# A transformer block with linear attention and a gated MLP: x^T of half the tiles by VectorE transposes of 4-byte elements and transfers inside SBUF

## The chip, the cores and the metric

The kernel runs on one core of a Trainium2 chip. The core has a matrix engine (TensorE, PE in the profile; its weight loads are listed as PEld), three engines for elementwise work (VectorE or DVE, ScalarE or ACT, GpSimd or POOL), a queue engine (SyncE or SP) and 16 DMA engines. Operands lie in SBUF, 128 partitions wide; TensorE writes to PSUM, eight banks of 128 x 512 fp32. The metric is the device time of one execution in microseconds. Lower is better.

## The reference

For 2048 tokens of width 448 (16 heads of 28) in bf16, with xn the layer norm of x:

```python
q, k, v = split(xn @ wqkv)                       # 448 -> 3 x 448
phi = lambda t: where(t > 0, t + 1, exp(t)) + 1e-6
kv  = sum over tokens of phi(k)^T v              # per head, 28 x 28
z   = sum over tokens of phi(k)
s   = (phi(q) @ kv) / (phi(q) . z + 1e-6) @ wo
g   = silu(relu(xn @ w1 + b1)^2 @ w2 + b2)       # 448 -> 1792 -> 448
out = x + s * g
```

No step mixes the order of the tokens: the sums run over all of them, and the rest is done token by token.

## The kernel before

The 2048 tokens are 16 tiles of 128 (`NT`), in four groups of four (`NG`). In memory token 4p + t of a group belongs to tile t, row p, for the groups 1 to 3.

A tile is loaded into `x_tok` (tokens on partitions), normalized into `xn` (512 columns: 448, and columns 448 to 511 repeat 384 to 447), and transposed into `xT` (features on partitions, four chunks of 128 features; the last chunk has the 64 remaining features twice, on both partition halves). Every product with the features as contraction reads `xT`:

- unit `K{tile}`: `xT` of a tile as weights, `w_k` moving, phi, into `pk`;
- unit `Q{group}.{m}`: `w_q` as weights, `xT` of four tiles moving, phi, into `pqT`;
- unit `H{group}.{fi}`: `w_1` as weights, `xT` of four tiles moving, bias, relu and square, into `r2`;
- gate `G{tile}`: 14 matmuls with `r2` of the tile as weights and `w_2` moving, then bias on VectorE into `gbuf`;
- sums `A{c}`: `xn` as weights and `pk` moving, from which kv follows; `S{tile}`: `pqT` as weights, the last attention product.

Contractions over 448 = 3 x 128 + 64 run in a 64-row mode: `pair` (line 591) puts two units on the two halves of the array, and `pe_four` (line 622) alternates two pairs. Gates run either alone, in the 128-row mode (`gg`, line 1013), or as a pair of two in the 64-row mode (`gate`, line 1237). The modes can't be mixed inside a run.

Transposes: tiles 0 to 3 at the start, singly; tiles 4 to 15 in pairs by `pe_transpose_two` (line 565, items `T4` to `T14` of the order). A pair is eight TensorE transposes into one PSUM bank (line 571, 128-row mode) and one eviction of 128 x 1024 by VectorE (line 583) or ScalarE (line 584). Ahead of it stand the statistics (line 459), the reciprocal root on ScalarE (lines 467 and 471), the normalization on VectorE (line 490) and the repeat of 64 columns (lines 512 and 513).

Order: TensorE and SP run in the order in which the program adds their work; for TensorE that is written by hand in the `run`, `gate` and `weave` strings from line 1240 on. A planner in Python (`schedule`, line 71) takes that order and places the work of VectorE, ScalarE and GpSimd by estimated durations and due times: an operation is due when its first reader is, less its duration (for a transfer, 4.5 us), and a PSUM bank should be read within 8 us. Some operations may go to one of two engines (`alts`). `emit` (line 221) turns the plan into fixed instruction lists with semaphore waits; each transfer has its own semaphore.

Queues: all loads of inputs are on SP, in the order of lines 423 to 452, with two small ones on ScalarE's queue. Later SP carries the reciprocal denominators to DRAM and back, and the outputs.

Of the kernel before, what the change touches and what calls it, by code (L numbers as in the profile page):

```python
# [9 lines left out]
P = 128  # L10
# [10 lines left out]
SWITCH = 0.095  # L21

# [7 lines left out]
class Op:  # L30
    def __init__(self, eng, emit, reads, writes, dur, alts, nbytes, mode, label):
# [7 lines left out]
        self.sync = None  # L39


class Program:
# [28 lines left out]
    def schedule(self):  # L71
        ops = self.ops
        t, mode = 0.0, None
        for op in ops:
            if op.eng == "pe":
                if op.mode != mode and mode is not None:
                    t += SWITCH
                mode = op.mode
                op.ideal = t
                t += op.dur  # L80
        for op in reversed(ops):
# [139 lines left out]
    def emit(self, nc, es):  # L221
        sems = {e: es.enter_context(nc.semaphore("q_" + e)) for e in self.ENGINES}
        n_dma = 0
        for e in self.ENGINES:
            k = 0
            for op in self.order[e]:
                if op.nbytes:
# [51 lines left out]
def bass_recurrent_scan__linear_attn_block__dense_activation_squared_relu__prompt_kernel(  # L279
    nc, A_x, A_wqkv, A_wo, B_x, B_w1, B_b1, B_w2, B_b2, out  # L280
):
    with ExitStack() as es:
# [44 lines left out]
        gbuf = sb("gbuf", [P, NT, D], bf)  # L327
        rB = xT[:, :, :, :].rearrange("p t c k -> p (t c k)")
# [157 lines left out]

        def ln_norm(si):
# [19 lines left out]
        def ln_twin(lo, hi):  # L507
            ts = range(lo, hi)

            def twin(e, eng):  # L510
                if eng == "dve":
                    return e.tensor_copy(xn[:, lo:hi, 448:512], xn[:, lo:hi, 384:448])
                return e.activation(out=xn[:, lo:hi, 448:512], in_=xn[:, lo:hi, 384:448], func=AF.Copy)
# [3 lines left out]
        MM = lambda n: n / 2400 + 0.0025  # L517

# [130 lines left out]
        def kk(si):  # L649
            b = Buf("K")  # L650

            def mm(e, rows, c, start, stop):
                return e.matmul(  # L653
                    ps(b)[:, 0:D], xT[rows, si, c, :], w_k[rows, c, :], start=start, stop=stop
                )

            return b, [("xT", si)] + wn("wk"), mm, lambda: phi(b, pk[:, si, :], ("pk", si), P, D, f"K{si}"), D, f"K{si}", 4

        def qq(g, m):
            b = Buf("Q")  # L660

            def mm(e, rows, c, start, stop):
                return e.matmul(  # L663
                    ps(b)[:, 0:512], w_q[rows, c, m * P : (m + 1) * P], xT[rows, 4 * g : 4 * g + 4, c, :],
# [3 lines left out]
            reads = [("xT", 4 * g + i) for i in range(4)] + wn("wq")  # L668
# [5 lines left out]
        unsquared = {}  # L674

# [25 lines left out]
        def hh(g, fi):  # L701
# [3 lines left out]
            def mm(e, rows, c, start, stop):  # L705
                return e.matmul(  # L706
                    ps(b)[:, 0:512], w_1[rows, c, fi * P : (fi + 1) * P], xT[rows, 4 * g : 4 * g + 4, c, :],
# [4 lines left out]
                b, [("xT", 4 * g + i) for i in range(4)] + names, mm, lambda: h_out(b, g, fi), 512, f"H{g}.{fi}", 4,  # L712
# [573 lines left out]
```

## Time and profile before

| | |
|---|---|
| runs | median 148.49 us of 3 (148.37 to 148.75) |
| profiled execution | 148.74 us, its span 147.0 us |
| granted TensorE clock | 0.998 |
| TensorE busy | 142.1 us (97%) |
| VectorE, ScalarE, GpSimd busy | 103.1, 79.9, 8.7 us |
| moved by DMA | 11.33 MB |

The span is the time from the first to the last instruction; the execution's time is 1.74 us longer. Times in the profile count from the start of the span. The profile's chain follows the work that ended last back from the end, at each step to what released it, and gives each stretch to an engine and a line. Matmuls are pipelined, so a single matmul's duration is longer than the step from one to the next; the chain's rows give the steps.

### The profile page before, as it was taken

The page shows a single profiled execution, that of the slowest core. Times are in us where ns is not written, and L with a number is a line of the kernel's source. Part 1 is how long each engine was busy: PE and PEld are TensorE (multiplying, and loading weights), DVE is VectorE, ACT ScalarE, POOL GpSimd, SP SyncE. Part 2 cuts the span into 40 slices and gives each one's busy share as a digit, 9 for nine tenths or more (in the row PEclk, how much of TensorE's full clock was granted, in tenths as well). Part 3 has the DMA queues.
Part 4 walks back from the last instruction along what each step waited for, and adds up shares of the span by engine and source line. Part 5 has one row for each costly group of instructions (what it writes and reads, how often), then busy time and mean ns, then how long its engine had stood idle before and what let it go on. Part 6 is the DMA issues. An engine that isn't in the chain of part 4 may idle for free.

```text
span 147.0 us, 3243 instructions
## 1 busy us (share of the span) xinstructions
PE 142.1 (97%) x1323; PEld 78.8 (54%) x1323; DVE 103.1 (70%) x225; ACT 79.9 (54%) x142; POOL 8.7 (6%) x44
## 2 busy tenths in 40 slices
PE   7799999999999999999999999999999999999991
PEld 7587455559564545544444444444556445555471
DVE  0742998993997898787989779872014755874874
ACT  3355898040768898538886167688427430301311
POOL 7680000000000000000000000000000000000000
PEclk9999999999999999999999999999999999999999
DMA  4999999400000000000000000000299300222032
GB/s 132 259 280 319 324 371 260 79 0 7 0 0 0 4 0 0 0 4 0 0 4 0 0 0 4 0 0 4 49 207 192 71 4 0 94 94 98 31 113 75
DMA packets 10315, 11.33 MB, mean 77 GB/s; under 512 B 1218, under 2 KB 9406, under 8 KB 10302
## 3 DMA queue, kind: packets, MB, share of 16 engines
q1 hardware_dynamic: 9458, 9.99, 24.3%
q10 hardware_dynamic: 844, 1.15, 3.4%
q8 instruction: 10, 0.16, 0.4%
q14 instruction: 3, 0.02, 0.0%
HBM read 9.23 MB, written 1.90 MB: 76 GB/s over the span
## 4 chain that ended last, share of the span: by engine, by line
PE 93%; DVE 3%; DMA 2%; ACT 0%; issue 0%
PE pb L706 26%; PE pb L1004 15%; PE pb L1021 11%; PE pb L1094 7%; PE pb L653 7%; PE pb L663 6%; PE pb L799 6%; PE pb L722 4%; PE pb L1059 3%; PE pb L571 2%; DMA x_tok<-in_A_x_dram 2%; PE pb L778 1%; DVE gbuf L1083 1%; PE pb L805 1%; PE pb L948 1%; PE pb L527 1%
## 5 line engine op out<-in xcount | busy, mean ns | idle before, releaser
L706 PE MATMUL pb<-xT,w 64*128 64x512 bf16 x350 | 41.5, 376 | 0.0
L684 ACT ACTIVATE r<-pb,b1f 128x512 bf16<-128x512 f32 x34 | 22.0, 687 | 10.9 <-PE pb L706 10.2
L706 PEld LDWEIGHTS pb<-xT,w 64*128 64x128 bf16 x350 | 17.4, 94 | 19.6 <-issue 0.4
L1004 PE MATMUL pb<-w,r 64*128 64x448 bf16 x224 | 23.1, 349 | 0.0
L681 DVE TENSOR_SCALAR r<-pb,b1f 128x512 bf16<-128x512 f32 x22 | 16.0, 745 | 4.7 <-PE pb L756 3.8
L696 ACT ACTIVATE r<-r 128x1024 bf16<-128x1024 bf16 x18 | 18.9, 1053 | 0.0
L1004 PEld LDWEIGHTS pb<-w,r 64*128 64x128 bf16 x224 | 11.9, 94 | 9.4 <-issue 0.4
L1021 PE MATMUL pb<-w,r 128*128 128x448 bf16 x84 | 16.7, 352 | 0.0
L653 PE MATMUL pb<-w_k,xT 64*128 64x448 bf16 x112 | 16.0, 349 | 0.0
L994 DVE TENSOR_TENSOR gbuf<-pb,b2b 128x448 bf16<-128x448 f32 x14 | 8.4, 620 | 8.2 <-PE pb L1004 4.7
L663 PE MATMUL pb<-xT,w_q 64*128 64x512 bf16 x84 | 13.8, 376 | 0.0
L1114 DVE TENSOR_TENSOR gbuf<-pb,gbuf 128x448 bf16<-128x448 f32 x14 | 8.1, 618 | 5.6 <-PE pb L1094 5.6
L1021 PEld LDWEIGHTS pb<-w,r 128*128 128x128 bf16 x84 | 8.0, 98 | 6.9
L1042 ACT ACTIVATE gbuf<-gbuf 128x448 bf16<-128x448 bf16 x14 | 7.0, 568 | 7.3 <-DVE gbuf L994 6.4
L459 DVE BATCH_NORM_STATS2 st<-x_tok 128x6 f32<-128x448 bf16 x16 | 9.2, 612 | 2.5 <-DMA x_tok<-in_A_x_dram 2.5
L1094 PE MATMUL pb<-w_k,pqT 64*128 64x448 bf16 x96 | 10.6, 349 | 0.0
L631 ACT ACTIVATE pk<-pb 128x448 bf16<-128x448 f32 x16 | 8.1, 540 | 4.1 <-PE pb L653 4.1
L912 DVE TENSOR_TENSOR pqT<-pqT,xT 128x2048 bf16<-128x2048 bf16 x3 | 3.7, 1222 | 9.2 <-DMA xT<-scr 9.2
L631 ACT ACTIVATE pqT<-pb 128x512 bf16<-128x512 f32 x12 | 6.7, 596 | 6.0 <-PE pb L663 5.5
L653 PEld LDWEIGHTS pb<-w_k,xT 64*128 64x128 bf16 x112 | 7.1, 94 | 5.0
L643 DVE SCALAR_TENSOR_TENSOR pk<-pb,pk 128x448 bf16<-128x448 f32 x16 | 9.5, 617 | 0.1
L799 PE MATMUL pb<-pk,xn 128*128 128x448 bf16 x48 | 9.4, 352 | 0.0
(98 smaller groups left out, 157.0 us busy)
## 6 DMA issues: line engine op xcount, KB each, us to landing
out_dram<-gbuf SPq DMA_DIRECT2D x15, 112.0 KB, 1.7
w<-in_B_w_dram SPq DMA_DIRECT2D x1, 1568.0 KB, 10.7
x_tok<-in_A_x_dram SPq DMA_DIRECT2D x3, 448.0 KB, 9.3
w<-in_B_w_dram SPq DMA_DIRECT2D x2, 384.0 KB, 5.9
xT<-scr SPq DMA_DIRECT2D x6, 112.0 KB
w<-in_B_w_dram SPq DMA_DIRECT2D x3, 192.0 KB, 3.8
xT<-scr ACTq DMA_DIRECT2D x5, 112.0 KB
w_o<-in_A_wo_dram SPq DMA_DIRECT2D x1, 392.0 KB, 9.3
```

The lines of the kernel that those rows point to most:

```text
L631: "act", lambda e, _: e.activation(out=slot, in_=ps(buf)[0:rows, 0:n], func=AF.Exp), [buf, "actw"],
L643: lambda e, _: e.scalar_tensor_tensor(out=slot, in0=ps(buf)[0:rows, 0:n], scalar=1.0 + 1e-6, in1=slot, op0=ALU.add, op1=ALU.max),
L653: return e.matmul(ps(b)[:, 0:D], xT[rows, si, c, :], w_k[rows, c, :], start=start, stop=stop)
L663: return e.matmul(ps(b)[:, 0:512], w_q[rows, c, m * P : (m + 1) * P], xT[rows, 4 * g : 4 * g + 4, c, :], start=start, stop=stop,)
L681: return e.tensor_scalar(out=slot, in0=ps(b)[:, 0:512], scalar1=b1f[:, fi : fi + 1], scalar2=0.0, op0=ALU.add, op1=ALU.max)
L684: return e.activation(out=slot, in_=ps(b)[:, 0:512], func=AF.Relu, bias=b1f[:, fi : fi + 1])
L696: return e.activation(out=both, in_=both, func=AF.Square)
L706: return e.matmul(ps(b)[:, 0:512], w_1[rows, c, fi * P : (fi + 1) * P], xT[rows, 4 * g : 4 * g + 4, c, :], start=start, stop=stop,)
L799: last = e.matmul(ps(b)[:, 0:D], xn[:, si, c * P : (c + 1) * P], pk[:, si, :], start=(si == 0), stop=(si == NT - 1),)
L1004: return e.matmul(ps(b)[:, 0:D], r2[rows, fi, si * P : (si + 1) * P], w_2[rows, fi, :], start=start, stop=stop)
L1021: last = e.matmul(ps(b)[:, 0:D], r2[:, fi, si * P : (si + 1) * P], w_2[:, fi, :], start=(fi == 0), stop=(fi == NF - 1),)
L1094: return e.matmul(ps(b)[:, 0:D], w, msb[rows, c, :], start=start, stop=stop)
```

## The change

Tiles 0 to 7 stay as they are. Tiles 8 to 15 (`SWAP = 2`, groups 2 and 3) take another way to `xT`:

- `xn` of two neighbouring tiles lies interleaved: column f of the even and of the odd tile are neighbours, and make up one 4-byte element. The normalization writes every second element (`xn_cols`).
- `dve_transpose` (items `X8` and `X12` of the order, in place of `T8`, `T10`, `T12` and `T14`): two VectorE instructions a group, each of 128 x 512 4-byte elements, transpose every 32 x 32 block in its place, into `stage` (for the second group, into the end of `gbuf`, not yet in use). Then 16 transfers on SP, one for each pair of 32-partition bands, move the blocks into `xT`: 32 partitions by 8 pieces of 128 bytes each. All 16 share one semaphore, and readers of the group wait for all of them.
- In `xT`, `pqT`, `pqR` and `r2` the columns of these groups keep the interleaved order. Where they move (Q and H) the group is one run of 512; where a tile of them is a weight (K, gates, S, and `xn` in the sums A) every second element is read.
- All normalizations of tiles 4 to 15 may go to ScalarE or VectorE (`ln_norm_either`), and read a product of mean and reciprocal root that GpSimd makes.
- In the planner the group's transfers are due 13 us ahead of their readers, and the first transpose 0.8 us earlier still.
- The order: gates 1, 2 and 3 run alone, in the 128-row mode, spread between the units of group 1, where gates 0 and 1 stood together and 2 and 3 were a pair. The rest of the order is as before.

```diff
+BANK_LATE = 8.0
+SWAP = 2
+PASSES = 1
...
-                late = min(late, s.ideal if s.eng == "pe" else s.late)
+                late = min(late, s.ideal if s.home == "pe" else s.late)
...
-                    late = min(late, self.writer[r].ideal + 8.0)
-            op.late = late - (4.5 if op.nbytes else op.dur + LAT[op.eng]) if op.prio is None else op.prio
+                    late = min(late, self.writer[r].ideal + BANK_LATE)
+            span = 13.0 if op.group else 4.5 if op.nbytes else op.dur + LAT[op.home]
+            op.late = late - span - op.lead if op.prio is None else op.prio
...
+                if op.group is not None:
+                    if op.group not in groups:
+                        groups[op.group] = es.enter_context(nc.semaphore(f"d{n_dma}")), ("d", n_dma)
+                        n_dma += 1
+                    op.sem, op.key = groups[op.group]
+                    op.seq = 16 * sum(o.group == op.group for o in self.ops)
+                elif op.nbytes:
...
+        stage = sb("stage", [P, 4, 4, 2, 64], bf)
...
+        def xn_cols(si, lo, hi):
+            if si < 4 * SWAP:
+                return xn[:, si, lo:hi]
+            pair_of = xn[:, si // 2 * 2 : si // 2 * 2 + 2, :].rearrange("p t f -> p (t f)")
+            return pair_of.rearrange("p (f t) -> p f t", t=2)[:, lo:hi, si % 2]
+
+        def columns(v, si):
+            if si < 4 * SWAP:
+                return v[:, si % 4 * P : si % 4 * P + P]
+            return v.rearrange("p (j k t) -> p j k t", j=2, t=2)[:, si % 4 // 2, :, si % 2]
+
+        def ln_norm_either(si):
+            add(
+                "pool",
+                lambda e, _: e.tensor_scalar(
+                    out=nmr[:, si : si + 1], in0=mv[:, si, 0:1], scalar1=rstd[:, si : si + 1], scalar2=-1.0,
+                    op0=ALU.mult, op1=ALU.mult,
+                ),
+                [("mv", si), ("rstd", si)], [("nmr", si)], 0.12, label=f"nm{si}",
+            )
+
+            def norm(e, eng):
+                if eng == "dve":
+                    return e.tensor_scalar(
+                        out=xn_cols(si, 0, D), in0=x_tok[:, si, :], scalar1=mv[:, si, 0:1],
+                        scalar2=rstd[:, si : si + 1], op0=ALU.subtract, op1=ALU.mult,
+                    )
+                return e.activation(
+                    out=xn_cols(si, 0, D), in_=x_tok[:, si, :], func=AF.Identity, scale=rstd[:, si : si + 1],
+                    bias=nmr[:, si : si + 1],
+                )
+
+            add(
+                "act", norm, [("x", si), ("mv", si), ("rstd", si), ("nmr", si)], [("xn", si)], 0.55, alts=[("dve", 0.39 if si < 4 * SWAP else 0.62)],
+                label=f"xn{si}",
+            )
...
+                if lo >= 4 * SWAP:
+                    both = xn[:, lo:hi, :].rearrange("p t f -> p (t f)")
+                    dst, src = both[:, 896:1024], both[:, 768:896]
...
+        def dve_transpose(lo):
+            first = lo == 4 * SWAP
+            parts = stage[:, :, :, :, :]
+            stays = [("stage", 0), ("stage", 1)]
+            if not first:
+                parts = gbuf[:, NT - 5 : NT, :].rearrange("p t f -> p (t f)")[:, 0:2048]
+                parts = parts.rearrange("p (b c j k) -> p b c j k", b=4, c=4, j=2)
+                stays += [("g", i) for i in range(NT - 5, NT)]
+            wide = parts.rearrange("p b c j k -> p (b c j k)").bitcast(f32)
+            wide = wide.rearrange("p (b c j k) -> p c b j k", b=4, c=4, j=2)
+            for j in range(2):
+                src = xn[:, lo + 2 * j : lo + 2 * j + 2, :].rearrange("p t f -> p (t f)").bitcast(f32)
+                src = src.rearrange("p (c b i) -> p c b i", c=4, b=4)
+                add(
+                    "dve", lambda e, _, j=j, src=src: e.transpose(wide[:, :, :, j, :], src),
+                    [(n, lo + 2 * j + t) for n in ("xn", "xd") for t in (0, 1)], [stays[j]] + (stays[2:] if j else []), 0.7, label=f"tr{lo + 2 * j}",
+                ).lead = 0.8 * (1 - j)
+            for a in range(4):
+                for b in range(4):
+                    src = parts[32 * a : 32 * a + 32, b, :, :, :].rearrange("p c j k -> p (c j) k")
+                    dst = by_group(slice(32 * b, 32 * b + 32), lo // 4).rearrange("p (n k) -> p n k", k=256)
+                    dma(
+                        "sp", dst[:, :, 64 * a : 64 * a + 64], src, [("xs", lo, a, b)], 32 * 1024,
+                        stays, dur=0.6, slow=1.5,
+                    ).group = ("xs", lo)
+
+        def by_group(rows, g):
+            return xT[rows, 4 * g : 4 * g + 4, :, :].rearrange("p t c k -> p (t c k)")
+
+        def x_group(rows, g, c):
+            if g < SWAP:
+                return xT[rows, 4 * g : 4 * g + 4, c, :]
+            return by_group(rows, g)[:, 512 * c : 512 * c + 512]
+
+        def x_tile(rows, si, c):
+            if si < 4 * SWAP:
+                return xT[rows, si, c, :]
+            return columns(x_group(rows, si // 4, c), si)
+
+        def x_reads(si, n=1):
+            if si >= 4 * SWAP:
+                return [("xs", si // 4 * 4, a, b) for a in range(4) for b in range(4)]
+            return [("xT", si + i) for i in range(n)]
...
-                    ps(b)[:, 0:D], xT[rows, si, c, :], w_k[rows, c, :], start=start, stop=stop
-                )
-
-            return b, [("xT", si)] + wn("wk"), mm, lambda: phi(b, pk[:, si, :], ("pk", si), P, D, f"K{si}"), D, f"K{si}", 4
+                    ps(b)[:, 0:D], x_tile(rows, si, c), w_k[rows, c, :], start=start, stop=stop
+                )
+
+            return b, x_reads(si) + wn("wk"), mm, lambda: phi(b, pk[:, si, :], ("pk", si), P, D, f"K{si}"), D, f"K{si}", 4
...
-                    ps(b)[:, 0:512], w_q[rows, c, m * P : (m + 1) * P], xT[rows, 4 * g : 4 * g + 4, c, :],
+                    ps(b)[:, 0:512], w_q[rows, c, m * P : (m + 1) * P], x_group(rows, g, c),
...
-            reads = [("xT", 4 * g + i) for i in range(4)] + wn("wq")
+            reads = x_reads(4 * g, 4) + wn("wq")
...
+        def r_cols(rows, fi, si):
+            g = si // 4
+            return columns(r2[rows, fi, g * 512 : (g + 1) * 512], si)
...
-                                ps(b)[:, 0:D], xn[:, si, c * P : (c + 1) * P], pk[:, si, :], start=(si == 0),
+                                ps(b)[:, 0:D], xn_cols(si, c * P, (c + 1) * P), pk[:, si, :], start=(si == 0),
...
-                            ps(b)[:, 0:D], r2[:, fi, si * P : (si + 1) * P], w_2[:, fi, :], start=(fi == 0),
+                            ps(b)[:, 0:D], r_cols(slice(0, P), fi, si), w_2[:, fi, :], start=(fi == 0),
...
-                w = pqT[rows, c, si * P : (si + 1) * P] if c < 3 else pqR[rows, g // 2, (si % 4) * P : (si % 4 + 1) * P]
+                w = columns(pqT[rows, c, g * 512 : (g + 1) * 512] if c < 3 else pqR[rows, g // 2, :], si)
...
-                ln_norm(si)
+                ln_norm_either(si)
...
+                elif w[0] == "X":
+                    dve_transpose(int(w[1:]))
...
-        run(hs(0, 6, 14) + " K0 K1 Q0.0 Q0.1 T4 G0 G1 T6 P8")
-        gate(2, 3, "K2", "K3", "Q0.2|K4")
-        run("H1.0 K5 H1.1 K6 H1.2 K7 H1.3 Q1.0 H1.4 Q1.1 H1.5 Q1.2 P12 " + hs(1, 6, 10) + " T8 T10 " + hs(1, 10, 14))
-        run("K8 H2.0 K9 H2.1 T12 G4 T14 G5 H2.2 K10 H2.3 K11 H2.4 Q2.0 H2.5 Q2.1")
+        run(hs(0, 6, 14) + " K0 K1 Q0.0 Q0.1 T4 G0 T6 P8")
+        run("G1 H1.0 K2 H1.1 K3 H1.2 K4 H1.3 K5 G2 X8 P12")
+        run("H1.4 H1.6 H1.5 H1.7 H1.8 Q0.2 H1.9 Q1.0 G3 H1.10 Q1.1 H1.11 Q1.2 H1.12 K6 H1.13 K7 X12")
+        run("K8 H2.0 K9 H2.1 G4 G5 H2.2 K10 H2.3 K11 H2.4 Q2.0 H2.5 Q2.1")

```

More of the change, by code (lines that the diff above doesn't have):

```diff
@@ L39, in __init__ @@
         self.sync = None
+        self.group = None
+        self.lead = 0.0
 class Program:
@@ L71, in schedule @@
     def schedule(self):
-        ops = self.ops
         t, mode = 0.0, None
-        for op in ops:
+        for op in self.ops:
+            op.home = op.eng
             if op.eng == "pe":
@@ L80, in schedule, with one_pass @@
                 t += op.dur
+        for k in range(PASSES):
+            self.one_pass()
+            if k < PASSES - 1:
+                for op in self.ops:
+                    if op.home == "pe":
+                        op.ideal = op.start
+                    op.start = op.end = None
+                    op.eng = op.home
+                    for b in op.writes:
+                        if isinstance(b, Buf):
+                            b.bank = None
+    def one_pass(self):
+        ops = self.ops
         for op in reversed(ops):
@@ L223, in emit @@
         n_dma = 0
+        groups = {}
         for e in self.ENGINES:
@@ L706, in mm @@
                 return e.matmul(
-                    ps(b)[:, 0:512], w_1[rows, c, fi * P : (fi + 1) * P], xT[rows, 4 * g : 4 * g + 4, c, :],
+                    ps(b)[:, 0:512], w_1[rows, c, fi * P : (fi + 1) * P], x_group(rows, g, c),
                     start=start, stop=stop,
@@ L711, in hh @@
             return (
-                b, [("xT", 4 * g + i) for i in range(4)] + names, mm, lambda: h_out(b, g, fi), 512, f"H{g}.{fi}", 4,
+                b, x_reads(4 * g, 4) + names, mm, lambda: h_out(b, g, fi), 512, f"H{g}.{fi}", 4,
             )
@@ L778, in f @@
                         last = e.matmul(
-                            ps(b)[64 * i : 64 * i + 64, 0:512], w, xT[:, 4 * g : 4 * g + 4, c, :], start=(c == 0), stop=(c == 3)
+                            ps(b)[64 * i : 64 * i + 64, 0:512], w, x_group(slice(0, P), g, c), start=(c == 0), stop=(c == 3)
                         )
@@ L783, in q_rest @@
             add(
-                "pe", f, [("xT", 4 * g + i) for g in ga for i in range(4)] + wn("wq") + ["wqh"], [b], 4 * MM(512),
+                "pe", f, [x for g in ga for x in x_reads(4 * g, 4)] + wn("wq") + ["wqh"], [b], 4 * MM(512),
                 mode="12864", label=f"QR{j}",
@@ L1004, in mm @@
                 return e.matmul(
-                    ps(b)[:, 0:D], r2[rows, fi, si * P : (si + 1) * P], w_2[rows, fi, :], start=start, stop=stop
+                    ps(b)[:, 0:D], r_cols(rows, fi, si), w_2[rows, fi, :], start=start, stop=stop
                 )
@@ L1059, in f @@
                     last = e.matmul(
-                        ps(b)[:, 0:n], r2[:, fi, si * P : (si + 1) * P], w_2[:, fi, lo:hi], start=(fi == 0 and not direct),
+                        ps(b)[:, 0:n], r_cols(slice(0, P), fi, si), w_2[:, fi, lo:hi], start=(fi == 0 and not direct),
                         stop=(fi == NF - 1),
```

10 lines of the change are left out of this document (5 added, 5 removed).

## The prediction

> **What bounds the kernel now.** I read the page first (span, busy shares, chain by engine), then the chain in order of time around the edited order, then the loads of VectorE and ScalarE in that stretch. The page:
>
> ```profile
> span 147.0 us, 3243 instructions
> PE 142.1 (97%) x1323; PEld 78.8 (54%) x1323; DVE 103.1 (70%) x225; ACT 79.9 (54%) x142; POOL 8.7 (6%) x44
> DMA  4999999400000000000000000000299300222032
> PE 93%; DVE 3%; DMA 2%; ACT 0%; issue 0%
> ```
>
> The chain is TensorE for 93% of the span. Transfers are absent from slice 9 to slice 28: the change puts its own into that empty stretch. The same chain in order of time (start, length, work):
>
> ```profile
> 22.92 0.55 PE pb L571 x8
> 23.48 5.30 PE pb L1021 x28
> 28.77 0.45 PE pb L571 x8
> 29.22 2.75 PE pb L1004 x28
> ...
> 33.59 2.65 PE pb L1004 x28
> ...
> 46.15 3.02 PE pb L706 x28
> 49.17 1.00 PE pb L571 x16
> 50.17 3.13 PE pb L706 x28
> 53.30 0.76 PE pb L653 x8
> ...
> 56.13 0.55 PE pb L571 x8
> 56.69 2.65 PE pb L1021 x14
> 59.34 0.45 PE pb L571 x8
> 59.78 2.65 PE pb L1021 x14
> 62.43 0.97 PE pb L706 x8
> ...
> 69.26 0.76 PE pb L653 x8
> ```
>
> No piece of another engine stands between these rows. So a microsecond of TensorE work taken out here comes off the span, as long as no new wait appears. The rows also price the order: a gate (14 matmuls, L1021) is 2.65; four H or Q units are 3.02; two H with two K are 56.13 - 53.30 = 2.83; a pair of tiles transposed costs 0.45; and entering another row mode costs 0.55 - 0.45 = 0.10, or 3.13 - 3.02 = 0.11. Gates 2 and 3, now one 64-row pair (2.75 and 2.65, L1004), cost the same as two gates at 2.65.
>
> **The change on TensorE.** T8, T10, T12 and T14 go. Walk the new order from 22.92: T4, G0, T6, G1 without a mode change inside, 0.55 + 2.65 + 0.45 + 2.65 = 6.30, to 29.22. Two groups of H1 with K2 to K5: 0.11 + 2 x 2.83, to 34.99. G2: 0.10 + 2.65, to 37.74. Two groups of four 512-column units: 0.11 + 2 x 3.02, to 43.89. G3: 2.75, to 46.64. One group of 3.02 and one with K6 and K7: 0.11 + 3.02 + 2.83, to 52.60, where K8 starts (53.30 before). K8's group, 2.83, to 55.43; G4 and G5: 0.10 + 5.30, to 60.83, where 62.43 stands before. The gain is 1.60: four transposed pairs at 0.45 give 1.80, and one more excursion into the 128-row mode takes back 0.2. After that the order is the same. Of this 1.60 nothing lies beside other work. Bounds: 1.8 if the extra mode change costs nothing, 1.4 if it costs twice.
>
> **The change on VectorE, ScalarE and GpSimd.**
>
> ```profile
> L490 DVE TENSOR_SCALAR xn<-x_tok,mv,rstd 128x448 bf16<-128x448 bf16 x15 | 5.3, 392 | 1.7 <-ACT rstd L471 1.6
> L583 DVE COPY xT<-pb 128x1024 bf16<-128x1024 bf16 x3 | 2.0, 684 | 0.4 <-PE pb L571 0.4
> L584 ACT ACTIVATE xT<-pb 128x1024 bf16<-128x1024 bf16 x3 | 3.1, 1021 | 4.4 <-PE pb L571 4.4
> L631 ACT ACTIVATE pk<-pb 128x448 bf16<-128x448 f32 x16 | 8.1, 540 | 4.1 <-PE pb L653 4.1
> L835 DVE TENSOR_TENSOR zacc<-zacc,pk 128x448 f32<-128x448 f32 x13 | 8.1, 622 | 0.3
> ```
>
> Removed: four of the six evictions of transposed pairs (0.68 on VectorE or 1.02 on ScalarE each), 2.7 to 4.1 in all. Added: four VectorE transposes, each of 512 four-byte elements a partition. No row shows one; the nearest is L835, 448 four-byte elements in 0.62, so by length 0.71. I bound it by 0.62 below and twice that row's rate, 1.42, above, and take 0.71: 2.8 for four (2.5 to 5.7). The normalizations of tiles 8 to 15 write every second element; if they stay on VectorE at the 448-element rate of L835 they cost 0.62 for 0.39, 8 x 0.23 = 1.8; on ScalarE some 0.54 each by L631. Twelve one-column products on GpSimd and one more hop ahead of each normalization of tiles 4 to 15 come with them. Together at most some 5 more than is taken out, and the cover for it is idle time beside TensorE:
>
> ```profile
> 23.00:29.20 6.20, 6.20 (x46) 3.54 (x46) 5.23 (x16) 2.64 (x6) 0.00 (x0) 1.00 0.75 146
> 29.20:38.00 8.80, 8.80 (x93) 6.28 (x94) 6.16 (x19) 3.37 (x9) 0.00 (x0) 1.00 0.01 3
> 38.00:53.30 15.30, 15.30 (x153) 8.12 (x150) 13.63 (x32) 11.99 (x21) 0.00 (x0) 1.00 0.00 1
> ```
>
> Columns: stretch, its length, busy TensorE, weight loads, VectorE, ScalarE, GpSimd, granted clock (1.00), DMA. From 29.2 to 38 the two engines idle 2.64 + 5.43 = 8.1 engine-microseconds, because gates leave them little to do; spreading gates 1 to 3 brings the evictions of H1.0 to H1.3 into that stretch, and takes them from the full one behind it. Over 23 to 53.3 they idle 5.3 + 12.3 = 17.6. I charge nothing. If that cover is gone, the first thing late is a PSUM bank that TensorE wants. T6 moves from 28.77 to 26.13 and needs tiles 6 and 7, of which this is the last step:
>
> ```profile
> 25.10 0.20 DVE L512 COPY xn<-xn 128x128 bf16<-128x128 bf16 x1
> ```
>
> It ends at 25.30, so 0.8 is left for the added hop. L490 already waits for the same reciprocal root, 1.6 in all over its waits; a hop of up to 0.8 is hidden, above it TensorE waits out the rest. I take nothing.
>
> **The transfers.** Each group of four tiles goes out as 16 transfers on SP's queue: 32 partitions by eight pieces of 128 bytes, 256 pieces over 16 DMA engines, so 256 pieces per engine and group. All 16 have one semaphore, and K8 (or K12) waits for the last.
>
> ```profile
> L400 SPq DMA_DIRECT2D w_k<-in_A_wqkv_dram x3: 487/507/732, 7.3 to 8.3; - x3
> L400 SPq DMA_DIRECT2D xT<-scr x11: 297/362/467, 104.9 to 108.8; - x11
> DMA to landing us min/median/max: 1.5/1.7/4.0
> q10 hardware_dynamic: 144, 0.07, 9.1%
> 19.17 1.16 SPq L400 DMA_DIRECT2D w_o<-in_A_wo_dram  x2
> 102.73 0.79 SPq L400 DMA_DIRECT2D scr<-rden  x2
> ```
>
> Issue: 0.36 by the eleven strided writes into xT (second row), 0.6 above by w_k's (mean 0.58), so 16 issues take 5.8 to 9.6. The fourth row is of the window 144.5 to 147: 144 packets, 128 of them of 512 bytes, in 9.1% of 16 x 2.5 us, 25 ns each. A 128-byte piece lies between a quarter of that, 6 ns, and all of it, so 256 take 1.6 to 6.5 on each engine, below the issue time. The issue sets the pace; with a landing of 1.5 to 4.0 (median 1.7, third row) a group needs 7.3 to 13.6. I take 0.5 per issue (between both rows, the shape being nearer w_k's) and the median: 9.7. SP has nothing else to do: its loads are issued by 20.3 and its next work starts at 102.73 (last two rows).
>
> When can it start? Rows of VectorE before:
>
> ```profile
> 32.30 1.31 DVE L490 TENSOR_SCALAR xn<-x_tok,mv,rstd 128x448 bf16<-128x448 bf16 x4
> 36.29 1.16 DVE L994 TENSOR_TENSOR gbuf<-pb,b2b 128x448 bf16<-128x448 f32 x2 [2.45 <-PE pb L1004]
> 57.47 0.70 DVE L490 TENSOR_SCALAR xn<-x_tok,mv,rstd 128x448 bf16<-128x448 bf16 x2 [0.43 <-ACT rstd L471]
> ```
>
> Tiles 8 to 11 are normalized by 33.6, with 2.45 idle before the next step. Add 0.9 for strided writes and 1.4 for two transposes: out by 36, landed by 45.7 (43.3 to 49.6), 7 ahead of K8 at 52.60. The second group is tighter. Tiles 14 and 15 end at 58.2 before, for a T14 at 59.34; left there, with 0.5 for strided writes and 1.4 for transposes it is issued from 60.0 and the group lands at 69.7, past K12's new start (69.26 - 1.60 = 67.66). But the planner gives the group a due time 13 ahead of its reader, and the normalization and transposes one before that, near 53, and it has all inputs on chip; VectorE and ScalarE have 1.7 + 3.3 idle in 38 to 53.3. I take transposes ending near 55 and landing near 65, and charge nothing. This is the thinnest cover of the sum.
>
> The Trainium skill has a rule against this step: "DMA: Bandwidth & Descriptors", its property table, wants 512 bytes a piece for line rate, with a read-modify-write below. The same page, "Why small descriptors are slow (HBM only)", exempts SBUF to SBUF, and no run shown here has such pieces. What the rule would make of the time stands under the first rival, from rows.
>
> **Strided weights.** K8 to K15, G8 to G15 and S8 to S15 load weights at every second element; x as the moving side becomes one run.
>
> ```profile
> L1021 PEld LDWEIGHTS pb<-w,r 128*128 128x128 bf16 x84 | 8.0, 98 | 6.9
> L948 PEld LDWEIGHTS pb<-at,w_v 128*112 128x112 bf16 x16 | 1.0, 132 | 0.1
> 112.38 1.28 PE pb L948 x28
> ```
>
> A load of 128 columns takes less (98 ns) than one of 112 (132): full loads run a faster path. In the 64-row mode two loads share the time of two concurrent matmuls, 2 x 2.65/28 = 0.19, so a load may stream up to 95 ns unseen. Lower bound: as now. If striding loses the fast path, the 132 ns of the 112-column row is mostly latency: the chain has 28 such loads (16 of 112 columns, 12 of 84, 100 on average) and their matmuls in 1.28, 46 ns each. At that rate 128 columns stream in 59 ns and stay hidden. I take nothing.
>
> **Sum.** The profiled execution took 148.74 (span 147.0 plus 1.74), 0.25 above the median 148.49. Its span less 1.60 is 145.4, its time 147.1; the median becomes 146.9.
>
> **Rivals.**
> 1. Slower: the second group lands late. One mechanism: 16 issues behind transposes that VectorE reaches late. Issued from 60.0, the group lands at 69.7 to 73.6, K12 waits 2.0 to 5.9, less 1.60: 148.9 to 152.8, middle 150.8. The gain is gone once the second transpose ends after 67.66 + 1.60 - 9.7 = 59.6 (55.7 at the slow end). With transposes in time at 55 but each piece at twice the 512-byte packet's 25 ns, a group takes 256 x 51 = 13 on the engines, lands with 1.5 more at 69.5, and K12 waits 1.8: 148.7. For: VectorE is busiest there; against: the due time. Chance 0.18.
> 2. Slower: strided weights stream at half the slow path's rate. The 59 ns above, doubled, are 118 against 95: 224 such loads in the 64-row mode, 23 ns each, 5.2 less 1.6: 152.1. Nothing in the rows speaks for a half rate, none shows a stride. Chance 0.08.
> 3. No change: the denser H1 and K stretch leaves banks late (or T6 waits), and TensorE stalls 1.2 to 2.0. Against: 17.6 idle. Chance 0.10, near 148.5.
> 4. Part of the gain: stalls of 0.4 to 1.1 from either cause: 147.3 to 148.0. Chance 0.12.
>
> **How the numbers follow.** The forecast has 0.52: 146.9, its own range 146.6 to 147.3. 0.3% (0.45 us) is about what a measurement of this kernel can tell from no change. Faster: forecast and case 4, 0.64. Same: case 3, 0.10. Slower: cases 1 and 2, 0.26. The range runs from 146.5 to 150.0: it leaves out case 2, the upper part of case 1 and a little below.
>
> **What would show it.** Right: no L571 after T6, 32 fewer transposes; K8 within 0.3 of 52.6 and its chain without DMA; SP issuing two runs of 16; four VectorE transposes near 0.7; weight loads of K8 at 94 to 98 ns. Wrong: the chain holding a DMA into xT ahead of K8 or K12, TensorE idle at T6 or at a bank, or L653's second half at more than 0.19 a pair.

## The result, and the profile after

The changed kernel takes 147.7 us (median of 5 runs, 147.04 to 147.76) against 148.49. The ratio is 0.9925, with a 95% interval of 0.9903 to 0.9946; it is an estimate over the executions and not the quotient of these two medians, which is 0.9947. Two further measurements gave 0.9908 (0.9873 to 0.9943) and 0.9930 (0.9903 to 0.9957). Ratios leave out executions that are over 1.5% slower than the fastest of their kernel. The kernel is faster, clear of noise: by 1.1, 1.4 and 1.0 us by these ratios and by 0.8 in the first medians, where 1.6 was forecast. The time lies inside the stated range.

The page of the changed kernel:

```profile
span 145.9 us, 3173 instructions
PE 140.2 (96%) x1263; PEld 74.0 (51%) x1263; DVE 101.9 (70%) x220; ACT 83.4 (57%) x147; POOL 11.7 (8%) x56
DMA  4999999300122202320000000000399200222132
PE 91%; DVE 4%; DMA 2%; ACT 1%; issue 0%
```

TensorE is still nearly the whole chain, 1.9 us shorter in busy time, and the stretch that had no transfers now has them. The chain in order of time:

```profile
14.27 6.04 PE pb L823 x56
...
23.18 0.55 PE pb L684 x8
23.73 2.65 PE pb L1138 x14
26.38 0.45 PE pb L684 x8
26.83 2.65 PE pb L1138 x14
...
35.25 2.75 PE pb L1138 x14
...
44.16 2.75 PE pb L1138 x14
...
52.31 1.32 PE pb L766 x14
53.63 0.00 issue
53.63 1.04 PE pb L823 x8
...
55.89 5.40 PE pb L1138 x28
61.29 0.97 PE pb L823 x8
...
68.12 0.76 PE pb L766 x8
...
137.40 4.30 PE pb L1176 x28
```

The first row is the first 64-row work, the H units of group 0; the last is the final gate. In the kernel before these two rows of the chain were:

```profile
14.02 6.04 PE pb L706 x56
...
138.54 4.30 PE pb L1059 x28
```

From the start of the one to the end of the other, which I call the body, the kernel before took 138.54 + 4.30 - 14.02 = 128.82 us and the changed one 137.40 + 4.30 - 14.27 = 127.43: 1.39 less. The head ahead of it is 0.25 longer in this execution. TensorE, VectorE, ScalarE and GpSimd do the same work there in the same order as before, and the granted clock was halved for a while (below, the last section). The body is the better measure here, since it leaves out the head, which differs from execution to execution by more than the effect.

Something is lost outside the span as well. An execution's time is longer than its span by 1.90 on average in this kernel (19 executions, 1.83 to 1.97) and by 1.74 in the kernel before (61 executions, 1.68 to 1.80). No run shows why.

The wait inside the body is at 53.63: H2.0's first eight matmuls take 1.04 where such a row takes 0.86. VectorE's order shows where it comes from:

```profile
50.08 0.71 DVE L602 STREAM_TRANSPOSE gbuf<-xn 128x512 f32<-128x512 f32 x1 [1.49 <-DMA xT<-stage]
...
52.77 0.71 DVE L798 TENSOR_SCALAR r<-pb,b1f 128x512 bf16<-128x512 f32 x1
```

The second group's first transpose stood 1.49 us for the first group's transfers, although it writes another area. The names tell why: `stays` holds the names of `stage` for both groups, so the planner saw a write to an area that is still being read. The relu behind it ends at 52.77 + 0.71 = 53.48, and H2.0's first weight load starts at 53.60 after 0.41 of idle time. The list of waits names no releaser for that idle time; that H2.0 waits for the bank which this relu frees is settled by e1 below.

The new work itself, by line:

```profile
L602 DVE STREAM_TRANSPOSE stage<-xn x2: 705/708/711, 34.8 to 36.3; 128x512 f32<-128x512 f32 x2
L428 SPq DMA_DIRECT2D xT<-stage x16: 610/612/1686, 37.1 to 48.1; - x16
DMA to landing us min/median/max: 1.9/1.9/3.1
L766 PEld LDWEIGHTS pb<-w_k,xT x112: 93/94/95, 19.9 to 72.4; 64*128 64x128 bf16 x112
L538 DVE TENSOR_SCALAR xn<-x_tok,mv,rstd x6: 381/446/537, 17.4 to 51.3; 128x448 bf16<-128x448 bf16 x6
L542 ACT ACTIVATE xn<-x_tok,nmr,rstd x6: 759/876/890, 24.2 to 50.3; 128x448 bf16<-128x448 bf16 x6
```

A VectorE transpose takes 0.71. An issue takes 0.61. The time to landing counts from the start of the issue (in e7's chain below the landing's row begins at 69.45, where the last issue starts), so the first group lands at 48.1 + 1.9 = 50.0, 12.9 us after its first issue and over 2 ahead of K8. Half of the K units' 112 weight loads read every second element, and all 112 take 93 to 95 ns. A normalization that writes every second element takes up to 0.54 on VectorE and up to 0.89 on ScalarE; the least times in these two rows, 0.38 and 0.76, are of tiles 4 to 7, whose writes are packed.

### The profile page after: what moved, and what is told of

Same layout as the page of the kernel before. It is cut to its first block, busy times and chain, and to the rows that moved or that the text cites. A ratio compares the mean times of both kernels' runs of the same rounds, so it can differ in the third digit from the quotient of the medians.

```text
span 145.9 us, 3173 instructions
## 1 busy us (share of the span) xinstructions
PE 140.2 (96%) x1263; PEld 74.0 (51%) x1263; DVE 101.9 (70%) x220; ACT 83.4 (57%) x147; POOL 11.7 (8%) x56
## 4 chain that ended last, share of the span: by engine, by line
PE 91%; DVE 4%; DMA 2%; ACT 1%; issue 0%
PE pb L823 26%; PE pb L1138 15%; PE pb L1121 11%; PE pb L1211 7%; PE pb L766 7%; PE pb L916 6%; PE pb L776 6%; PE pb L1176 3%; PE pb L839 3%; DMA x_tok<-in_A_x_dram 2%; PE pb L895 1%; DVE st L487 1%; DVE gbuf L1200 1%; PE pb L922 1%; PE pb L1065 1%; PE pb L684 1%
## 5 line engine op out<-in xcount | busy, mean ns | idle before, releaser
L1138 PE MATMUL pb<-w,r 128*128 128x448 bf16 x112 | 22.4, 353 | 0.0
L813 ACT ACTIVATE r<-r 128x1024 bf16<-128x1024 bf16 x21 | 21.8, 1055 | 0.0
L798 DVE TENSOR_SCALAR r<-pb,b1f 128x512 bf16<-128x512 f32 x23 | 16.6, 742 | 6.1 <-PE pb L873 4.2
L1121 PE MATMUL pb<-w,r 64*128 64x448 bf16 x168 | 17.4, 349 | 0.0
L1138 PEld LDWEIGHTS pb<-w,r 128*128 128x128 bf16 x112 | 10.6, 98 | 10.4 <-issue 0.4
L766 PE MATMUL pb<-w_k,xT 64*128 64x448 bf16 x112 | 14.4, 349 | 0.0
L1121 PEld LDWEIGHTS pb<-w,r 64*128 64x128 bf16 x168 | 8.1, 94 | 8.0 <-issue 0.4
L776 PE MATMUL pb<-xT,w_q 64*128 64x512 bf16 x84 | 12.0, 376 | 0.0
L766 PEld LDWEIGHTS pb<-w_k,xT 64*128 64x128 bf16 x112 | 6.2, 94 | 5.8
L952 DVE TENSOR_TENSOR zacc<-zacc,pk 128x448 f32<-128x448 f32 x13 | 8.1, 621 | 0.3
```

The source lines that it names most:

```text
L766: return e.matmul(ps(b)[:, 0:D], x_tile(rows, si, c), w_k[rows, c, :], start=start, stop=stop)
L776: return e.matmul(ps(b)[:, 0:512], w_q[rows, c, m * P : (m + 1) * P], x_group(rows, g, c), start=start, stop=stop,)
L798: return e.tensor_scalar(out=slot, in0=ps(b)[:, 0:512], scalar1=b1f[:, fi : fi + 1], scalar2=0.0, op0=ALU.add, op1=ALU.max)
L813: return e.activation(out=both, in_=both, func=AF.Square)
L1121: return e.matmul(ps(b)[:, 0:D], r_cols(rows, fi, si), w_2[rows, fi, :], start=start, stop=stop)
L1138: last = e.matmul(ps(b)[:, 0:D], r_cols(slice(0, P), fi, si), w_2[:, fi, :], start=(fi == 0), stop=(fi == NF - 1),)
```

## The experiments

Two theories stood at the start. Mine: the time follows TensorE's order (0.45 for a pair of tiles, 0.2 for an excursion into the 128-row mode), and what is missing is the head and the 0.17 at H2.0. The rival: the spreading of the gates does the work, by evening out the evictions, or is needed to make room.

**The changed kernel again**, twice, beside the others.

> The changed kernel once more, as the measure for its neighbours. Both theories: ratio to the kernel before 0.992 +- 0.003; single times between 147.0 and 147.8. If the head of the profiled execution (half the granted clock from 7.3 to 11 us there) was an accident of that execution, its chain reaches the first H unit of group 0 in 64-row mode near 14.0, not 14.3, and the rest of the chain keeps its steps.

> The changed kernel beside e1's kernel on one chip, to size the false wait. Theory: the chain of the profiled execution shows 0.1 to 0.3 us of waiting between K8 and G4 that e1's does not, and the ratio to the kernel before is 0.990 to 0.993, 0.001 to 0.003 above e1's. Rival (no difference): both ratios within 0.001.

Measured: 147.38 (ratio 0.9908) and 147.41 (0.9930), bodies 127.42 and 127.42, so the body repeats to 0.01 while single times spread from 146.68 to 149.57, wider than expected. The wait at H2.0 is in both chains. The first 64-row work did not begin near 14.0, but at 16.09 and 14.83: the late head was no accident of one execution. Nor does it belong to the change, since e1's kernel has the same head and began that work at 14.01 and 13.87.

**e1: own names for the second group's staging area.**

```diff
-                stays += [("g", i) for i in range(NT - 5, NT)]
+                stays = [("stage", 2), ("stage", 3)] + [("g", i) for i in range(NT - 5, NT)]
```

> The second group's staging area gets names of its own, so that its first transpose no longer waits for the first group's transfers, which read another area. Theory (TensorE's order sets the time; that wait only delays one bank): the 1.5 us wait on VectorE near 48.6 goes, H2.0 starts right behind K8, and the time falls by 0.1 to 0.2 against the changed kernel. Rival (the false wait is what keeps the change from its 1.6): the time falls by 0.5 to 0.7, to 146.9 to 147.1.

> The changed kernel with own names for the second group's staging area, once more. Theory: ratio to the kernel before 0.988 to 0.990 (148.49 - 1.60 is 0.9892), no piece of another engine on the chain from the first 64-row group to the last gate. Rival (e1 was a lucky run): 0.991 to 0.993 as the changed kernel.

Measured: 146.84, ratio 0.9883 (0.9856 to 0.9910), and again 147.35, 0.9919 (0.9895 to 0.9942). Its chain:

```profile
53.37 0.86 PE pb L823 x8
...
55.45 5.40 PE pb L1138 x28
60.85 0.97 PE pb L823 x8
...
67.68 0.76 PE pb L766 x8
```

The wait at H2.0 is gone, 0.86 for 1.04. With the head of the kernel before (14.01 here) H2.2 starts at 60.85, where the prediction's walk put 60.83, and K12 at 67.68 against 67.66. The body is 127.25 in both measurements, 1.57 under the kernel before. So the false wait cost 0.17 of the body, as the theory had it, and not 0.5 to 0.7. The times alone would not tell. In the first comparison the medians of e1 and the changed kernel differ by 0.54, which is the rival's figure; in the second they differ by 0.06, and e1's 0.9919 lies where the rival of a lucky run put it. The ratios differ by 0.0025 and 0.001, far less than the width of their intervals. It is the chains and the bodies, the same in both measurements, that decide.

**e2: the spreading alone** (`SWAP = 4`, so that no tile takes the new way; the normalization on either engine and the new order of group 1's units stay).

```diff
...
-        run("H1.4 H1.6 H1.5 H1.7 H1.8 Q0.2 H1.9 Q1.0 G3 H1.10 Q1.1 H1.11 Q1.2 H1.12 K6 H1.13 K7 X12")
-        run("K8 H2.0 K9 H2.1 G4 G5 H2.2 K10 H2.3 K11 H2.4 Q2.0 H2.5 Q2.1")
+        run("H1.4 H1.6 H1.5 H1.7 H1.8 Q0.2 H1.9 Q1.0 G3 T8 T10 H1.10 Q1.1 H1.11 Q1.2 H1.12 K6 H1.13 K7")
+        run("K8 H2.0 K9 H2.1 T12 G4 T14 G5 H2.2 K10 H2.3 K11 H2.4 Q2.0 H2.5 Q2.1")
```

> Only the spreading of gates 1 to 3 (and the normalization on either engine): all tiles are transposed on TensorE again, T8 and T10 behind G3, T12 and T14 around G4 as before. Theory (TensorE's order sets the time): four pairs at 0.45 come back and one excursion into the 128-row mode more than in the kernel before stays, so 148.49 + 0.2 = 148.7, ratio 1.001. Rival (the spreading gains by itself, since it evens out the evictions): 147.5 to 148.2, ratio 0.993 to 0.998.

Measured: ratio 1.0008 (0.9985 to 1.0030), body 129.04, 0.22 over the kernel before. In its chain T8 and T10, now behind G3 without a mode change of their own, take

```profile
45.86 0.89 PE pb L684 x16
```

that is 0.45 a pair. The spreading by itself gains nothing and costs one excursion; the rival in its first form falls, since 0.993 to 0.998 lies outside the interval.

**e3 and e4: the transposes alone**, gates 0 to 3 as in the kernel before; e4 has own names besides.

```diff
-        run(hs(0, 6, 14) + " K0 K1 Q0.0 Q0.1 T4 G0 T6 P8")
-        run("G1 H1.0 K2 H1.1 K3 H1.2 K4 H1.3 K5 G2 X8 P12")
-        run("H1.4 H1.6 H1.5 H1.7 H1.8 Q0.2 H1.9 Q1.0 G3 H1.10 Q1.1 H1.11 Q1.2 H1.12 K6 H1.13 K7 X12")
-        run("K8 H2.0 K9 H2.1 G4 G5 H2.2 K10 H2.3 K11 H2.4 Q2.0 H2.5 Q2.1")
+        run(hs(0, 6, 14) + " K0 K1 Q0.0 Q0.1 T4 G0 G1 T6 P8")
+        gate(2, 3, "K2", "K3", "Q0.2|K4")
+        run("X8 H1.0 K5 H1.1 K6 H1.2 K7 H1.3 Q1.0 H1.4 Q1.1 H1.5 Q1.2 P12 " + hs(1, 6, 14))
+        run("X12 K8 H2.0 K9 H2.1 G4 G5 H2.2 K10 H2.3 K11 H2.4 Q2.0 H2.5 Q2.1")
```

> Only the VectorE transposes and transfers: gates 0 and 1 together and 2 and 3 as a pair, as in the kernel before, T8 to T14 left out. Theory (TensorE's order sets the time): four pairs at 0.45 and one excursion at 0.2 go, 148.49 - 2.0 = 146.5, ratio 0.9865, unless K8 (due at 52.2) or K12 (due at 67.3) waits for transfers. Rival (the spreading is needed to make room for the transposes): TensorE waits 0.5 to 2 ahead of K8 or H2, 147.0 to 148.5.

> As e3 (gates as in the kernel before, no TensorE transposes of tiles 8 to 15), with the second group's staging area under its own names. In e3 TensorE waited 1.8 us for a bank of a Q unit whose last step stood behind the second group's normalization and transpose in VectorE's queue. Theory A (with gates 0 to 3 bunched there is no room for that work in 45 to 52, whatever the plan): the wait stays at 1 to 2, 147.9 to 148.6, ratio 0.995 to 1.000. Theory B (the false wait distorted the planner's order, room is there): no wait on the chain, 148.5 - 2.0 = 146.5, ratio 0.985 to 0.989.

Measured: e3 148.48, ratio 0.9989 (0.9968 to 1.0010), body 128.78; e4 149.14, 1.0034 (1.0016 to 1.0052), body 128.78. Of the 2.0 that TensorE's order saves, all but 0.04 is given back, 1.8 of it in one wait (e3, the list of waits):

```profile
PE pb L823 <- DVE pqT L756: 1.8, 1, 1.8
```

and in VectorE's order ahead of it:

```profile
49.84 0.54 DVE L538 TENSOR_SCALAR xn<-x_tok,mv,rstd 128x448 bf16<-128x448 bf16 x1 [0.81 <-POOL nmr L529]
50.27 0.70 DVE L602 STREAM_TRANSPOSE gbuf<-xn 128x512 f32<-128x512 f32 x1
50.90 1.25 DVE L756 SCALAR_TENSOR_TENSOR pqT<-pb,pqT 128x512 bf16<-128x512 f32 x2
```

The second group's normalization and transpose, due early for transfers that take 13 us, stand ahead of the last step of two Q units, whose banks TensorE wants; VectorE waits 0.81 there for GpSimd's product. That wait isn't needed either: the VectorE form of the normalization reads the mean and the reciprocal root, and only the ScalarE form reads the product. The root was ready at 49.21 in ScalarE's order, so the normalization could have started some 0.6 sooner, an estimate; no run takes this wait out with the gates bunched. The false wait on the staging area has no part in it (e4). So the rival's second form holds: with the gates bunched, this plan doesn't find the room. Whether room is missing or only the due time too early, e3 and e4 can't say; e9 does.

**e5: as e1, gates 2 and 3 as one pair.**

```diff
-        run("G1 H1.0 K2 H1.1 K3 H1.2 K4 H1.3 K5 G2 X8 P12")
-        run("H1.4 H1.6 H1.5 H1.7 H1.8 Q0.2 H1.9 Q1.0 G3 H1.10 Q1.1 H1.11 Q1.2 H1.12 K6 H1.13 K7 X12")
+        run("G1 H1.0 K2 H1.1 K3 H1.2 K4 H1.3 K5 X8 P12")
+        gate(2, 3, "H1.4", "H1.5", "H1.6|H1.7")
+        run("H1.8 Q0.2 H1.9 Q1.0 H1.10 Q1.1 H1.11 Q1.2 H1.12 K6 H1.13 K7 X12")
```

> As e1 (own names), and gates 2 and 3 run as one pair in the 64-row mode between H1.4 and H1.7, in place of two gates alone. Theory (an excursion into the 128-row mode costs 0.2, evictions keep up): two excursions go, 0.4 under e1, ratio to the kernel before 0.984 to 0.987, near 146.4. Rival (two gates at a stretch leave too little room for the evictions, as in e3): TensorE waits 0.5 to 2, ratio 0.988 to 0.998.

Measured: 148.43, ratio 0.9980 (0.9958 to 1.0002), body 128.26, 1.0 over e1. TensorE waits 1.3 us for one relu on ScalarE, as the rival had it. In ScalarE's order that relu stands behind two normalizations, of which this is the second:

```profile
35.54 0.89 ACT L542 ACTIVATE xn<-x_tok,nmr,rstd 128x448 bf16<-128x448 bf16 x1
36.29 0.66 ACT L801 ACTIVATE r<-pb,b1f 128x512 bf16<-128x512 f32 x1
```

The planner costs such a normalization at 0.55; it takes 0.89, so the two explain some 0.7 of the 1.3 at most, an estimate. A pair of gates asks for two banks at once, which may be the rest; e9 has such a pair at another place and no wait there, so this isn't shown.

**e6: as e1, the transfers due 8 us ahead instead of 13.**

```diff
-            span = 13.0 if op.group else 4.5 if op.nbytes else op.dur + LAT[op.home]
+            span = 8.0 if op.group else 4.5 if op.nbytes else op.dur + LAT[op.home]
```

> As e1, but the planner has the transfers due 8 us ahead of their reader instead of 13. A group takes 12.9 from its first issue to its last landing in e1. Theory (the due time is what holds the second group ahead of K12): its transposes come up to 5 later, K12 waits 1 to 3, 148 to 150. Rival (VectorE has idle time and takes the work early anyway): no wait, within 0.3 of e1, ratio 0.986 to 0.991.

Measured: 151.23, ratio 1.0163 (1.0126 to 1.0199), body 130.94, 3.7 over e1, and more than the 148 to 150 expected, because both groups are late and not the second alone:

```profile
PE pb L766 <- DMA xT<-stage: 2.1, 1, 2.1
PE pb L766 <- DMA xT<-gbuf: 1.2, 1, 1.2
```

The due time of 13 is what keeps the transfers off the chain, for the first group as well.

**e7: as e1, eight transfers more in the second group.** They write the first group's old staging area and add nothing to the result.

```diff
+                    if not first and b < 2:
+                        spare = stage[32 * b : 32 * b + 32, :, :, :, :].rearrange("p b c j k -> p (b c j k)")
+                        dst = spare.rearrange("p (n k) -> p n k", k=256)
+                        dma(
+                            "sp", dst[:, :, 64 * a : 64 * a + 64], src, [("spare", a, b)], 32 * 1024,
+                            stays + [("xs", 8, i, j) for i in range(4) for j in range(4)], dur=0.6, slow=1.5,
+                        ).group = ("xs", lo)
```

> As e1, with eight transfers more in the second group, of the same shape, into the first group's staging area, under the same semaphore; they add nothing to the result. In e1 the last of the second group lands near 65.0 and K12 starts at 67.7, so 2.7 are to spare. Theory (the issue on SP sets the pace, 0.61 to 0.68 each): 5 to 5.4 more, K12 waits 2.3 to 2.7, time 2.3 to 2.7 over e1, 149.1 to 149.6, ratio 1.003 to 1.007. Rival (the transfers overlap, landing is paced by the DMA engines at 0.25 busy): under 1 more, no wait, ratio as e1.

Measured: 151.05 (150.99 to 151.22), ratio 1.0167 (1.0139 to 1.0196), body 129.09, 1.84 over e1's. The chain holds the 24 issues, one every 0.65, and ends in the wait:

```profile
16.09 6.04 PE pb L830 x56
...
69.45 1.93 DMA xT<-gbuf
71.38 0.05 issue
71.42 0.93 PE pb L773 x8
```

The price is of the expected kind: beyond its slack a group's lateness goes into the time. K12 waits 1.7 by the list of waits, and not 2.3 to 2.7, because the expectation put e1's last landing near 65.0. Counted from the start of the last issue it was at 64.25, so 3.4 were to spare; with the head's 2.08 taken off, eight more issues landed the group 5.05 later, which leaves a wait of 1.6. The median lies 1.5 to 2 above the expectation; in the profiled execution that is the head, 2.1 late (16.09). For the other three executions it isn't shown. Their granted clock is 0.987 to 0.989 against 0.977, so their heads were hardly the same, and why they took as long stays open.

**e8: as e1, tiles 4 to 15 normalized on VectorE alone** (the planner takes 0.55 for a strided one).

```diff
-                ln_norm_either(si)
+                ln_norm(si)
...
-                    out=xn[:, si, 0:D], in0=x_tok[:, si, :], scalar1=mv[:, si, 0:1],
+                    out=xn_cols(si, 0, D), in0=x_tok[:, si, :], scalar1=mv[:, si, 0:1],
```

> As e1, but tiles 4 to 15 are normalized on VectorE alone, as in the kernel before, still with every second element written for tiles 8 to 15. Theory (VectorE's fixed order is what e3 to e5 ran into): six normalizations of 0.54 more on VectorE ahead of the phis in 45 to 53, TensorE waits 0.3 to 2 for a bank, ratio 0.990 to 1.001. Rival (either engine has room): no wait, ratio as e1, 0.987 to 0.990.

Measured: 146.75, ratio 0.9877 (0.9856 to 0.9899), body 127.25 to the digit of e1's. My theory fell: VectorE has room for six more normalizations once the gates are spread, and the part that lets ScalarE help gains nothing here. Its ratio is the lowest measured, though the intervals of e1 and e9 overlap with its own and e9's body is shorter. Of what its time gains over e1, 0.17 lies outside the span: time and span differ by 1.73 here, as in the kernel before, and by 1.90 in e1.

**e9: as e4, every second transfer issued by GpSimd, SP's due 8.5 us ahead.**

```diff
-            span = 13.0 if op.group else 4.5 if op.nbytes else op.dur + LAT[op.home]
+            span = 8.5 if op.group else 4.5 if op.nbytes else op.dur + LAT[op.home]
...
-                        "sp", dst[:, :, 64 * a : 64 * a + 64], src, [("xs", lo, a, b)], 32 * 1024,
+                        ("sp", "pool")[b % 2], dst[:, :, 64 * a : 64 * a + 64], src, [("xs", lo, a, b)], 32 * 1024,
...
-                    ).group = ("xs", lo)
+                    ).group = None if b % 2 else ("xs", lo)
```

> As e4 (gates bunched as in the kernel before), but every second transfer is issued by GpSimd, and the transfers on SP are due 8.5 us ahead. SP then issues 8 a group, 5.2 us, and lands 7 after the first issue. Theory (in e3 and e4 the early due time put the second group's work ahead of a phi in VectorE's queue): with the later due time the wait for that bank goes or shrinks below 0.5, and if GpSimd issues as fast as SP nothing waits: 146.5 to 147.2. Rival (GpSimd issues slower than SP, or there is no room at all): K8 or K12 waits for a transfer issued by GpSimd, or a bank is late again, 148 to 152.

Measured: 147.07, ratio 0.9887 (0.9860 to 0.9914), body 126.83, 1.99 under the kernel before: the 2.0 that e3 was to give. GpSimd issues as fast as SP (4.85 for eight), and where e3 waited nothing stands now: VectorE starts the second group's normalizations at 55.7, where in e3 they started at 48.1, ahead of the Q units' last steps. The first fence is GpSimd's order, the second the chain:

```profile
36.23 4.85 POOL L428 DMA_DIRECT2D xT<-stage  x8 [2.04 <-DVE stage L602]
```

```profile
46.09 6.04 PE pb L823 x56
52.13 0.76 PE pb L766 x8
```

So the bunched gates do leave room. In e3 and e4 it was the early due time, which 16 issues on one queue ask for, that put the second group's work in the way. Spreading the gates is one way out, a shorter group the other. e9 changes issue and due time together; that the second alone would not do is only suggested by e6.

## Why the prediction was right

- **TensorE's order, 1.60.** Right. The body fell by 1.57 in e1 and by 1.39 in the changed kernel. The prices hold one by one: 0.45 a pair (e2), 0.2 an excursion (e2, +0.22), 2.0 without the extra excursion (e9, 1.99). H2.2 and K12 start in e1 within 0.02 of where the walk put them.
- **Edits costed at nothing.** Here is the step that failed: "I take transposes ending near 55 and landing near 65, and charge nothing", with no wait between the groups. I read the staging area of the second group as its own, as its bytes are, and overlooked that it kept the first one's names. The first thing late was a PSUM bank, as the prediction said of a lost cover, and the cost is 0.17 of the body. A second term was put at nothing without a reason: the 1.74 between span and time was carried over, and is 1.90 in the changed kernel.
- **The cover.** Right in sum: in the changed kernel's busy times of the same stretches VectorE and ScalarE together have 4.5 more, of the "some 5" that were allowed (columns as before; ScalarE rose from 3.37 to 6.05 and from 11.99 to 14.10):

```profile
29.20:38.00 8.80, 8.80 (x74) 3.99 (x74) 7.39 (x21) 6.05 (x14) 0.99 (x4) 1.00 0.00 1
38.00:53.30 15.30, 15.30 (x135) 6.92 (x134) 12.13 (x28) 14.10 (x24) 0.99 (x4) 1.00 0.21 36
```

  But idle time in sum isn't room in an engine's order: e3 had as much of it (9.7 in these stretches against 8.5 here) and waited 1.8 behind two instructions. The argument from summed idle time was too weak for the conclusion, and only the spread order made it true.
- **VectorE's transposes** were taken at 0.71 and take 0.71. The strided normalization was mis-sized for ScalarE: 0.54 taken, up to 0.89 measured; the wait in the changed kernel doesn't lie behind it, and in e5 it is part of the 1.3.
- **The transfers.** Issue-bound, as forecast. 0.61 an issue, 0.65 from one to the next and 1.7 for one in each group, where 0.5 was taken, so a group needs 12.9 and not 9.7, near the upper bound of 13.6. That the second group landed at 65.7, near the 65 taken, is luck: its transposes ended at 52.9 and not near 55. One row of e1, the window from 36 to 70, gives the pieces:

```profile
q1 hardware_dynamic: 8704, 1.05, 18.5%
```

  0.185 x 16 x 34 us over 8704 packets (8192 pieces of 128 bytes, and 16 more for each transfer) is 11.6 ns each, between the bounds of 6 and 25, and far below the 51 of the first rival's second mechanism. By the byte a piece is still dearer than a 512-byte packet: 128 bytes in 11.6 ns are 11 bytes a ns, against 20. The Trainium skill ("DMA: Bandwidth & Descriptors", property table) wants 512 bytes for line rate, with a read-modify-write below, and the same page ("Why small descriptors are slow (HBM only)") says that transfers inside SBUF don't suffer from small pieces. The 11.6 shows no price of a read-modify-write above the 25 ns, and the bytes a ns show that the rate of larger packets isn't reached either.
- **The first rival** (the second group late) had the right place and price: e6 and e7 make it happen, and the planner's due time is what excludes it. In the changed kernel the group lands near 65.7 (its last issue starts at 63.77) and K12 starts at 68.12, so 2.4 were to spare.
- **Strided weights** cost nothing: 93 to 95 ns in all K loads, and the steps of gates and S units are the same 2.65 and 1.32 as before.
- **The size.** Of the 1.60, the false wait took 0.17 and the time outside the span 0.16. The body's 1.39 less 0.16 gives 1.2, and the three ratios are falls of 1.1, 1.4 and 1.0. In the first measurement the medians fell by 0.8 only; the head was 0.25 later in its profiled execution, and single executions spread over 0.7. The median of 147.7 lies outside the forecast's own 146.6 to 147.3 and inside case 4's 147.3 to 148.0, but case 4's stalls of 0.4 to 1.1 did not come, only one of 0.17. The stated range held the result because the rivals had widened it.

## What to carry to other kernels

Where one engine is the whole chain, price its order row by row, mode changes included: such a sum came out to 0.03 us of the body here once the false wait on the chain was gone. Before calling an added step hidden, look for the instruction that will stand behind it in that engine's fixed order, and at how early a slow transfer forces the step to be due; summed idle time doesn't answer that. A buffer that is tracked by name has to get a new name when its place changes, and an operation that may go to one of two engines should wait only for what its form on that engine reads.

## What the runs showed of the hardware

TensorE's granted clock in the first microseconds decides up to 2 us. In the changed kernel and in e7, the windows of one microsecond from 10 to 11 (granted clock in the third column from the end):

```profile
10.00:11.00 1.00, 1.00 (x14) 1.00 (x12) 0.00 (x0) 0.49 (x1) 0.77 (x4) 0.60 0.91 303
```

```profile
10.00:11.00 1.00, 1.00 (x11) 1.00 (x11) 0.10 (x1) 0.67 (x2) 0.86 (x3) 0.50 1.03 346
```

In the kernel before it is 1.00 there. In the changed kernel the clock is at 0.5 from about 7.4 to 10.8 and the 64-row work starts at 14.27; in e7 it is at 0.5 from about 7.4 until after 14 and that work starts at 16.09; with the full clock it started at 13.8 to 14.1 in eight profiled executions and at 13.2 in a ninth, e2's. One pair isolates the clock: in e1 and in the second execution of the changed kernel the chain reaches TensorE's line 839 at 9.09 and 9.13, and the 64-row work starts at 14.01 with the full clock and at 16.09 with the halved one. The Trainium skill ("TensorE: Matmul & The Clock Gate", on the free-running window) has it that the same kernel can meet the gate at another phase in each run, and the three executions of the changed kernel, with 14.27, 16.09 and 14.83, agree: the clock is halved there for about 3.4, 6.8 and 3.4 us.

Writing every second of 448 elements cost VectorE and ScalarE about the same on top, 0.1 to 0.15 us, and ScalarE was the slower place for it as for the packed write: 0.86 to 0.89 against 0.50 to 0.54 strided, 0.76 against 0.38 packed.
